# A gated linear attention with an MLP behind it: k of the first unit moves to SyncE's queue, and the first two v loads arrive as bf16

## The chip, the core and the metric

The kernel runs on one core of a Trainium2 chip. The metric is the device time of one execution in microseconds (us). Six kinds of hardware matter here. TensorE (PE in the profile) multiplies matrices, and its weight loads have a row of their own, PEld. VectorE (DVE) and ScalarE (ACT) work on elements. GpSimd (POOL) does little arithmetic here, but it issues most of the loads. SyncE (SP) issues loads and stores. Sixteen DMA engines move the data of all queues.

## The reference, cut to what matters

There are two stages. The first is a recurrent attention over 768 steps for 4 batches of 8 heads, with a decay `alpha` for each channel of the state. The second is an MLP with a tanh GELU over the 3072 tokens that come out.

```python
for t in range(S):                       # B, H, S, D = 4, 8, 768, 48
    state = alpha[:, :, t, :, None] * state + einsum('bhd,bhe->bhde', k[:, :, t], v[:, :, t])
    y[:, :, t] = einsum('bhd,bhde->bhe', q[:, :, t], state)
x = y.transpose(0, 2, 1, 3).reshape(B * S, H * D)      # 3072 x 384
h = x @ w_in                                           # 384 x 2048
out = gelu_tanh(h) @ w_out                             # 2048 x 384
```

All inputs and the output are float32.

## The kernel before

**Chunks, pairs and units.** The 768 steps are cut into six chunks of 128. A chunk of two batches is a pair, so there are twelve pairs, numbered 0 to 11; pairs 0 and 1 are chunk 0 of batches 0 and 1, and of batches 2 and 3. One batch of a pair is called a unit here. A task's name is its kind, the pair and a running number: `kp0.0` is the task `kp` of the first unit of pair 0, `kp0.1` that of the second unit.

**What a unit does.** Its decays go through a logarithm (`ln`, ACT), a running sum by a triangular matrix (`cum`, PE) and exponentials (`b`, `binv`, `bend`, ACT). VectorE forms `qp` = q times b and `kp` = k times binv (line 451). TensorE transposes both (`t`, line 461), ACT or DVE copies them out of PSUM (`ev`, line 479), TensorE forms the scores (`attn`, line 555), and VectorE masks them (`mask`, line 562). Then TensorE multiplies the masked scores with v (`y`, line 612), and the transposed-back keys with v (`kv`, line 572), from which VectorE makes the state (`st`, line 597). The result is copied (`x`), transposed (`tx`, line 643) and copied again (`xe`, line 647), and is then the input of the MLP: `l1` (line 655, weights `w_in`), `gelu` (ACT) and `l2` (line 674, weights `w_out`).

**Order.** Each engine runs its instructions in a fixed order. For the opening this order is written out by hand in `FIRST`: each word has an engine letter (P TensorE, V VectorE, A ScalarE, G GpSimd, S SyncE) and a task. `P:fill.3` is three products of zeros that keep TensorE running. After the list a planner orders the rest with costs and due times. TensorE's opening goes, cut to what matters, `cum0.0 cum0.1 t0.0 t0.1 attn0.0 t0.2 t0.3 t0.4 attn0.1 t0.5 cum1.0 y0.0 kv0.0 cum1.1 tx0.0 y0.1 t1.1 t1.0 kv0.1 tx0.1 attn1.0 t1.2 l10.0`. An instruction that waits holds up all that stand behind it on its engine.

**The loads.** There are two ways in. `RINGS` lists the twelve loads of a, q and k of pairs 0 and 1, one batch each, 192 KB; SP issues them, or ACT those named in `BY_ACT`. They are numbered `load.0` to `load.11` in the order of `RINGS`: a0.0, a0.1, q0.0, k0.0, q0.1, k0.1, then the same of pair 1. These are hardware queues: q1 in the profile is SP's, q10 is ACT's. All other loads, those of v and of the weights among them, are issued by GpSimd on a software queue, q0, in the order of `LOADS`. This queue can change the type on the way, and the weights and most v loads come as bf16 by it. The names of the first ones are `load.12` (v of pair 0), `load.13` (`w_in` part 0), `load.14` (v of pair 1), `load.15` to `load.17` (`w_in` parts 1 to 3) and then `w_out`. Two `gate` tasks hold GpSimd back: `load.12` may go once a0.1 has landed (`gate.0`), and what stands behind it once k0.1 has landed (`gate.1`); a gate is a small copy on GpSimd that reads the loaded tile (line 338).

**v.** For the pairs in `NARROW` v is loaded as float32 into a buffer of the pool `a`, and four `vb` tasks (line 422), one for each unit, copy it to a bf16 tile of the pool `vb`. For all other pairs the load itself writes the `vb` tile. In `load`, the line that decides is

```python
t = "vb" if n == "v" and u["m"] not in self.NARROW else n
u[t] = self.tile("a" if t == "v" else t, [C, 2, H, D], BF16 if t == "vb" else F32, t)
```

where `u["m"]` is the pair. `LANDED` holds times that the planner takes for the landings; it is the same in both kernels.

Of the kernel before, what the change touches and what calls it, by code (L numbers as in the profile page):

```python
# [174 lines left out]
class _Kernel:  # L175
# [8 lines left out]
    PACKED, CUM_FF, R = (0, 1), (0, 1), 4  # L184
    RINGS = (('a', 0, 0, 1), ('a', 0, 1, 2), ('q', 0, 0, 1), ('k', 0, 0, 1), ('q', 0, 1, 2), ('k', 0, 1, 2),
             ('a', 1, 0, 1), ('a', 1, 1, 2), ('q', 1, 0, 1), ('k', 1, 0, 1), ('q', 1, 1, 2), ('k', 1, 1, 2))
    BY_ACT = (2, 3,)

    FIRST = """
        A:table.0 A:load.2 A:load.3 S:load.0 S:load.1 S:load.4 A:ln0.0 S:load.5 P:fill.7 P:cum0.0 A:ln0.1 G:gate.0 G:load.12 S:load.6 P:cum0.1 A:b0.0 S:load.7  # L190
        A:bend0.0 V:qp0.0 A:binv0.0 A:binv0.1 S:load.8 V:kp0.0 P:fill.2 P:t0.0 A:b0.1 V:ev0.0 P:fill.1 P:t0.1 S:load.9 A:ev0.1 V:qp0.1 S:load.10 A:bend0.1
        P:fill.3 P:attn0.0 V:kp0.1 G:gate.1 S:load.11 P:t0.2 G:load.13 V:mask0.0 A:ev0.2 P:t0.3 G:load.14 V:mask0.1 A:ev0.3 P:fill.1 P:t0.4 V:ev0.4 P:fill.1
        P:attn0.1 A:ln1.0 G:load.15 P:t0.5 V:mask0.3 P:cum1.0 A:ev0.5 G:load.16 V:vb0.0 A:ln1.1 V:end0.0 P:y0.0 V:mask0.2 G:load.17 P:kv0.0 A:binv1.0 P:cum1.1
        V:st0.0 A:x0.0 G:load.18 A:vb0.1 V:kp1.0 P:tx0.0 A:b1.0 P:y0.1 V:xe0.0 G:load.19 V:qp1.0 P:t1.1 A:x0.1 A:bend1.0 G:load.20 A:b1.1 P:fill.1 P:t1.0
        A:ev1.0 V:ev1.1 G:load.21 V:qp1.1 P:fill.1 P:kv0.1 V:st0.1 G:load.22 A:binv1.1 P:tx0.1 P:attn1.0 V:xe0.1 G:load.23 P:t1.2 V:kp1.1 P:l10.0 A:ev1.2
        G:load.24 V:mask1.0 P:t1.3 A:bend1.1 P:t1.4 V:mask1.1 G:load.25 A:ev1.3 P:l10.1 V:ev1.4 G:load.26 A:vb1.0 P:t1.5 P:attn1.1 G:load.27 V:ev1.5 P:y1.0
        G:load.28 P:l10.3 V:end1.0 V:vb1.1 V:mask1.2 G:load.29 A:gelu0.0 P:kv1.0 P:l10.2 V:mask1.3 A:x1.0 G:load.30 P:l10.5 A:gelu0.1 V:st1.0 A:gelu0.3 P:y1.1
        G:load.31 P:l10.4 A:gelu0.5 V:x1.1 P:tx1.0 A:gelu0.2 P:tx1.1 P:l10.6 G:load.32 V:xe1.1 A:gelu0.4 V:xe1.0 P:l10.7 A:gelu0.6 G:load.33 P:l11.0 A:gelu0.7
        P:l11.6 A:gelu1.0 P:l11.5 A:gelu1.6 P:l11.7 A:gelu1.5 P:l11.2 A:gelu1.7 P:l11.4 A:gelu1.2 P:l11.3 A:gelu1.4 P:l11.1 A:gelu1.3 P:kv1.1 P:l20.0
        A:gelu1.1 P:l20.4 P:l20.1 A:ln2.0 P:l20.2 P:cum2.0 P:l20.5 A:b2.0 A:binv2.0 P:l20.9 A:bend2.0 V:kp2.0 A:ln2.1 P:l20.6 V:st1.1 P:cum2.1 V:qp2.0 P:l20.8  # L200
# [8 lines left out]
              27900, "load.23": 28300, "load.24": 30100, "load.25": 31000, "load.26": 31900, "load.27": 32600, "load.28": 32900, "load.29":  # L209
              34800, "load.30": 36700, "load.31": 38400, "load.32": 41200, "load.33": 42600}  # L210

    NARROW = (0, 1)

    TURN_QK = (7,8,9,10,11)

# [101 lines left out]
    def load(self, n, c, i, lo=0, hi=2):  # L317
# [4 lines left out]
        def emit(e):  # L322
            t = "vb" if n == "v" and u["m"] not in self.NARROW else n
            if t not in u:
                u[t] = self.tile("a" if t == "v" else t, [C, 2, H, D], BF16 if t == "vb" else F32, t)
            dma = {"SP": nc.sync, "ACT": nc.scalar}.get(e, nc.gpsimd).dma_start
            src = self.src[n][2 * i + lo:2 * i + hi]
            if u["packed"] and n != "v":
                dma(u[n][:, lo].rearrange("p (o r) d -> p o (r d)", o=2),
                    src[0, :, c * C:(c + 1) * C].rearrange("h (g r) d -> g h (r d)", r=R))  # L330
            else:
                dma(u[t][:, lo:hi].rearrange("t b h d -> t (b h) d"), src.rearrange("b h s d -> s (b h) d")[c * C:(c + 1) * C])  # L332
# [369 lines left out]
    def tasks(self):  # L702
# [9 lines left out]
        def load(key, cost, emit):  # L712
            nonlocal n
            land = W[key[1] if key[0] == "w" else "cast" if key[0] == "v" and key[1] not in self.NARROW else "strip"]
            loads[key] = s.add("load", {"POOL": cost}, n, emit, gate, land=land * 3 // 8 if key[0] != "w" and key[1] in self.SPLIT else land)
# [17 lines left out]
        for r, m, lo, hi in self.RINGS:  # L733
            loads[r, m, lo] = loads[r, m, hi - 1] = s.add(
                "load", {"ACT" if n in self.BY_ACT else "SP": W["ring_issue"]}, n, self.load(r, *pairs[m], lo, hi), land=(W["ring_v" if r == "v" else "ring"] * (hi - lo) // 2 if n else W["begin"]))
            n += 1
# [22 lines left out]
        for m, (c, i) in enumerate(pairs):  # L759
# [61 lines left out]
            vin = [loads["v", m, j] for j in range(2)]  # L821
            if m in self.NARROW:
                vin = [s.add("vb", {"DVE": W["vb"], "ACT": W["vb_act"]}, P + 19, self.narrow(u, j, j + 1), vin[j:j + 1]) for j in range(2)]
# [87 lines left out]
            kp[0].take("kp", *tq, *kvs)  # L911
            if m in self.NARROW:
                loads["v", m, 0].take("a", *vin)
# [129 lines left out]
```

## Time and profile before

| | us |
|---|---|
| median of 3 runs | 175.16 (174.92 to 175.46) |
| the profiled execution | 175.79 |
| its span, first to last instruction | 174.0 |
| PE busy in the span | 168.1 (97%) |
| ACT, DVE, POOL busy | 129.2, 95.0, 58.2 |
| PE busy from 0 to 17 us | 14.11 of 17 |
| DMA: 28.88 MB in the span | mean 166 GB/s |

The times of the profile are counted from the start of the span. 1.8 us of the profiled execution lie outside of it, and this execution was 0.6 us longer than the median. The clock that TensorE was granted is full (1.00) in every stretch. A busy PE counts the products of zeros too, 17 of which stand in the opening. The opening lasts until the first product of the MLP, which starts 17.06 us into the span.

The landings of the opening's loads, as issue time plus time to landing in the trace's list of DMA issues, each asked for in a window around its issue:

| load | issued by, at | lands at | first read |
|---|---|---|---|
| a0.0, a0.1 | SP 0.74, 1.4 | 3.7, 4.7 | `ln0.0` 3.74, `ln0.1` 4.75 |
| q0.0 | ACT 1.20 | 4.2 | `qp0.0` 5.77 |
| k0.0 | ACT 1.92 | 7.5 | `kp0.0` 7.57 |
| q0.1, k0.1 | SP 2.19, 2.86 | 7.7, 8.2 | `qp0.1` 8.65, `kp0.1` 9.11 |
| v of pair 0 | POOL 4.90 | 11.5 | `vb0.0` 12.24 |
| `w_in` part 0 | POOL 8.79 | 14.8 | `l10.0` 17.06 |
| v of pair 1 | POOL 9.52 | 16.0 | `vb1.0` 18.62 |
| `w_in` part 1 | POOL 10.71 | 18.3 | `l10.3` 19.68 |
| `w_in` part 2 | POOL 11.5 | 20.5 | `l10.5` 21.2 |
| `w_in` part 3 | POOL 12.2 | 22.2 | `l10.6` 23.03 |

### The profile page before, as it was taken

To read this page: it belongs to the slowest core of one execution; us is meant where nothing else is said; L and a number is where in the kernel's file an instruction comes from. 1 tells how busy PE (TensorE), PEld (TensorE's weight loads), DVE (VectorE), ACT (ScalarE), POOL (GpSimd) and SP (SyncE) were. 2 spreads that over 40 slices of the span, in tenths; PEclk is the share of its full clock that TensorE was granted. 3 is DMA by queue.
4 is the path that set the end of the run, shared out by engine and by line. 5 is a ranking of instruction groups with operands and counts; after the bars stand their busy time and mean duration, and the time that the engine had idled before them with its cause. 6 is when DMAs were issued, how large, how long until landed. Compare 5 with 4: busy or idle time off the path is not lost.

```text
span 174.0 us, 4688 instructions
## 1 busy us (share of the span) xinstructions
PE 168.1 (97%) x1973; PEld 132.2 (76%) x1973; DVE 95.0 (55%) x188; ACT 129.2 (74%) x217; POOL 58.2 (33%) x67
## 2 busy tenths in 40 slices
PE   7799999999999999999999999999999999999993
PEld 2466999666887896797698697788697796886973
DVE  6399920265967864865995866587464520420000
ACT  4578999765979759959889697968799693481931
POOL 2398346995735667572000028000203000000000
PEclk9999999999999999999999999999999999999999
DMA  4999999999999999999952367999895843202102
GB/s 138 292 271 217 201 247 227 234 223 203 238 285 194 241 254 221 231 235 192 214 162 52 98 160 177 161 172 161 77 138 100 88 127 86 92 23 68 49 0 90
DMA packets 49621, 28.88 MB, mean 166 GB/s; under 512 B 37696, under 2 KB 46016, under 8 KB 49600
## 3 DMA queue, kind: packets, MB, share of 16 engines
q0 software_dynamic: 26464, 17.70, 62.6%
q1 hardware_dynamic: 22592, 10.49, 26.1%
q10 hardware_dynamic: 544, 0.39, 0.9%
q8 instruction: 15, 0.25, 0.7%
q14 instruction: 6, 0.05, 0.1%
HBM read 25.17 MB, written 4.72 MB: 172 GB/s over the span
## 4 chain that ended last, share of the span: by engine, by line
PE 86%; DMA 8%; ACT 3%; DVE 0%; issue 0%; SPq 0%; DVEq 0%
PE hT L655 36%; PE acc L674 33%; DMA xT<-x 5%; PE at L555 3%; DMA k<-in_k_dram 3%; PE qkT_ps L461 2%; PE cum L411 2%; PE yps L620 2%; PE kv L572 1%; PE qkT_ps L492 1%; PE yps L535 1%; PE xT_ps L643 1%; PE yps L612 1%; ACT qkT L479 1%; PE k_ps L507 1%; ACT L304 1%
## 5 line engine op out<-in xcount | busy, mean ns | idle before, releaser
L655 PE MATMUL hT<-xT,w_in 128*128 128x256 bf16 x576 | 68.3, 273 | 0.4 <-DMA xT<-x 0.4
L674 PE MATMUL acc<-w_out,gT 128*128 128x384 bf16 (+3 forms) x416 | 68.7, 313 | 0.0
L661 ACT ACTIVATE gT<-hT 128x512 bf16<-128x512 f32 x96 | 55.3, 601 | 13.1 <-PE hT L655 9.7
L655 PEld LDWEIGHTS <-w_in 128*128 128x128 bf16 x576 | 61.3, 114 | 2.6 <-DMA xT<-x 0.8
L674 PEld LDWEIGHTS <-gT 128*128 128x128 bf16 x416 | 37.0, 98 | 19.4
L562 DVE TENSOR_TENSOR atm<-at,ut 128x512 bf16<-128x512 f32 x48 | 30.2, 684 | 19.1 <-PE at L555 18.9
L686 ACT COPY ot<-acc 128x384 f32<-128x384 f32 (+3 forms) x18 | 7.9, 442 | 16.7 <-PE acc L674 15.9
L451 DVE TENSOR_TENSOR kp<-k,binv 128x768 bf16<-128x768 f32 (+1 forms) x15 | 11.9, 791 | 11.8 <-ACT binv L440 10.6
L346 POOL CAST gate<-qkT 128x1 f32<-128x1 bf16 x3 | 0.6, 183 | 45.0 <-DMA qkT<-kp 45.0
L332 POOL DMA_DIRECT2D k<-in_k_dram x11 | 12.2, 1107 | 8.4 <-DMA vb<-in_v_dram 4.4
L451 DVE TENSOR_TENSOR qp<-q,b 128x768 bf16<-128x768 f32 (+1 forms) x15 | 11.9, 793 | 4.4 <-ACT b L440 4.3
L332 POOL DMA_DIRECT2D vb<-in_v_dram x11 | 12.1, 1104 | 6.0 <-DMA w_in<-in_moe_w_in_dram 1.5
L332 POOL DMA_DIRECT2D a<-in_alpha_dram x11 | 12.2, 1113 | 4.9 <-DMA w_in<-in_moe_w_in_dram 1.3
L332 POOL DMA_DIRECT2D q<-in_q_dram x11 | 12.2, 1109 | 4.0 <-DMA w_out<-in_moe_w_out_dram 1.0
L440 ACT ACTIVATE b<-cum 128x768 bf16<-128x768 f32 (+1 forms) x15 | 10.3, 684 | 3.2 <-PE cum L411 1.6
L304 ACT ACT_TABLE_LOAD x9 | 11.5, 1283 | 0.9 <-PEq L1027 0.7
L630 DVE CAST x<-yps 128x384 bf16<-128x384 f32 x10 | 5.4, 556 | 12.2 <-PE yps L620 12.2
L661 ACT ACT_TABLE_LOAD x9 | 11.5, 1283 | 0.2
L594 DVE TENSOR_TENSOR stmp<-kv,st 128x384 f32<-128x384 f32 x16 | 8.9, 553 | 4.8 <-PE kv L572 4.7
L440 ACT ACTIVATE binv<-cum 128x768 bf16<-128x768 f32 (+1 forms) x15 | 10.3, 684 | 0.1
L597 DVE TENSOR_TENSOR st<-stmp,ends 128x384 bf16<-128x384 f32 x16 | 8.9, 558 | 0.6
L479 ACT COPY qkT<-qkT_ps 128x512 bf16<-128x512 bf16 (+1 forms) x8 | 5.4, 693 | 4.6 <-PE qkT_ps L461 4.5
(79 smaller groups left out, 155.2 us busy)
## 6 DMA issues: line engine op xcount, KB each, us to landing
out_dram<-ot SPq DMA_DIRECT2D x19, 192.0 KB, 4.2
a<-in_alpha_dram POOLq DMA_DIRECT2D x9, 384.0 KB, 11.8
q<-in_q_dram POOLq DMA_DIRECT2D x9, 384.0 KB, 11.2
k<-in_k_dram POOLq DMA_DIRECT2D x9, 384.0 KB, 11.5
vb<-in_v_dram POOLq DMA_DIRECT2D x9, 192.0 KB, 11.4
w_in<-in_moe_w_in_dram POOLq DMA_DIRECT2D x4, 384.0 KB, 8.3
w_out<-in_moe_w_out_dram POOLq DMA_DIRECT2D x4, 384.0 KB, 11.0
out_dram<-ot SPq DMA_DIRECT2D x9, 96.0 KB, 3.2
```

Of the source, the lines that this page charges most:

```text
L304: nc.scalar.add_instruction(mybir.InstLoadActFuncSet(name=nc.get_next_instruction_name(), act_func_set_id=i, engine=mybir.EngineType.Activ ...
L332: dma(u[t][:, lo:hi].rearrange("t b h d -> t (b h) d"), src.rearrange("b h s d -> s (b h) d")[c * C:(c + 1) * C])
L440: self.nc.scalar.activation(u[n].rearrange("t i h d -> t i (h d)")[:, lo:hi], cum, AF.Exp, scale=1.0 if n == "b" else -1.0)
L451: self.nc.vector.tensor_tensor(out, rows, b, op=ALU.mult)
L479: self.copy(e)(t, ps)
L562: self.nc.vector.tensor_tensor(u["atm", i][:, o], u["at", i][o], self.ut[:, None, :].to_broadcast([self.C, self.H // 2, self.C]), op=ALU.mult)
L594: nc.vector.tensor_tensor(s, acc, old, op=ALU.add)
L597: nc.vector.tensor_tensor(new.rearrange("f p (o d) -> f (p o) d", o=2), acc.rearrange("f p (o d) -> f (p o) d", o=2), ends, op=ALU.mult)
L655: self.nc.tensor.matmul(h[:, s], w_in[:, j, nt % 4 + s], self.xT[c % self.NX][:, j, lo:hi].rearrange("p g t -> p (g t)"), start=j == 0, st ...
L661: return lambda e: self.nc.scalar.activation(self.gT[c % self.NG][:, nt:nt + 2, lo * self.C:hi * self.C], f.pop(("h", c, lo, nt)), AF.Gelu ...
L674: self.nc.tensor.matmul(f["acc", c, b][:, lo:hi], self.gT[c % self.NG][:, nt, b * self.C:(b + 1) * self.C], self.w_out[:, nt, lo:hi], star ...
L686: self.copy(e)(f["ot", c, b][:, sl], f["acc", c, b] if half is None else f["acc", c, b, half][:, sl])
```

## The change

Two things change. `BY_ACT` loses load 3, so k0.0 is issued by SP, third in its queue: behind the two alpha loads of pair 0 and ahead of q0.1. ACT's queue has one load left, q0.0. `NARROW` is empty, so the v loads of pairs 0 and 1 write bf16 tiles themselves, and the four `vb` tasks are gone: two of VectorE (`vb0.0`, `vb1.1`) and two of ScalarE (`vb0.1`, `vb1.0`). The words `A:load.3` and those of the four `vb` tasks leave `FIRST`, and `S:load.3` enters it; the rest of it is the same.

```diff
-    BY_ACT = (2, 3,)
+    BY_ACT = (2,)
     FIRST = """
-        A:table.0 A:load.2 A:load.3 S:load.0 S:load.1 S:load.4 A:ln0.0 ...
+        A:table.0 A:load.2 S:load.0 S:load.1 S:load.3 S:load.4 A:ln0.0 ...
...
-        P:attn0.1 A:ln1.0 G:load.15 P:t0.5 V:mask0.3 P:cum1.0 A:ev0.5 G:load.16 V:vb0.0 A:ln1.1 V:end0.0 P:y0.0 ...
+        P:attn0.1 A:ln1.0 G:load.15 P:t0.5 V:mask0.3 P:cum1.0 A:ev0.5 G:load.16 A:ln1.1 V:end0.0 P:y0.0 ...
-        V:st0.0 A:x0.0 G:load.18 A:vb0.1 V:kp1.0 ...
+        V:st0.0 A:x0.0 G:load.18 V:kp1.0 ...
...
-        ... A:ev1.3 P:l10.1 V:ev1.4 G:load.26 A:vb1.0 P:t1.5 P:attn1.1 G:load.27 V:ev1.5 P:y1.0
+        ... A:ev1.3 P:l10.1 V:ev1.4 G:load.26 P:t1.5 P:attn1.1 G:load.27 V:ev1.5 P:y1.0
-        G:load.28 P:l10.3 V:end1.0 V:vb1.1 V:mask1.2 ...
+        G:load.28 P:l10.3 V:end1.0 V:mask1.2 ...
...
-    NARROW = (0, 1)
+    NARROW = ()
```

What follows from it on each queue: TensorE has the same instructions in the same order, and `y0.0`, `y0.1` and `y1.0`, which waited for the `vb` tasks, now wait for the DMA. SP issues eleven loads in the opening instead of ten, ACT one instead of two. GpSimd issues the same loads; since v of pairs 0 and 1 takes no buffer of the pool `a` any more, the v load of pair 7 stands four places earlier, ahead of the alpha, q and k loads of pair 8 and the alpha load of pair 9, and some of its waits are for other loads or engines.

## The prediction

> **What bounds the kernel now.** I read the busy times by stretch first, then the chain of waits, then the timeline of the opening, and last the list of DMA issues. The stretches (us, then busy time of PE, PEld, DVE, ACT and POOL, granted clock, DMA share, GB/s) are
>
> ```profile
> 0.00:17.00 17.00, 14.11 (x150) 8.37 (x151) 12.45 (x42) 10.74 (x24) 10.54 (x21) 1.00 0.92 231
> 17.00:24.00 7.00, 7.00 (x95) 6.68 (x93) 5.58 (x13) 6.49 (x13) 2.52 (x4) 1.00 1.17 204
> ```
>
> From 17 us on TensorE is full, and it stays so nearly to the end: its only listed wait after 17 us is 0.4 us. So the program ends a fixed time after `l10.0` starts (17.06), and the change is worth what it moves that start by, unless the MLP then waits for its weights. The DMA engines are full too, so a load that gains takes from another. The chain of waits (start, length, what) runs through k0.0:
>
> ```profile
> 1.92 5.55 DMA k<-in_k_dram
> ...
> 7.57 0.57 DVE kp L451
> 8.14 0.05 issue
> 8.19 0.40 PE qkT_ps L461 x4
> ...
> 13.71 0.42 ACT vb L422
> 14.13 0.04 issue
> 14.18 0.36 PE yps L612 x8
> ```
>
> It shows both targets of the change: a 5.55 us load, and a 0.42 us narrowing. The timeline (start, length, engine, line, instruction) has what stands around them:
>
> ```profile
> 4.90 1.29 POOL L332 DMA_DIRECT2D v<-in_v_dram  x1
> ...
> 12.24 0.35 DVE L422 CAST vb<-v 128x384 bf16<-128x384 f32 x1
> ...
> 12.41 0.24 PE L383 MATMUL cum<-blk,la 128*128 128x4 f16 x4
> ...
> 12.65 0.37 PE L612 MATMUL yps<-vb,atm 128*128 128x48 bf16 x8
> ```
>
> v of pair 0 takes 6.6 us to landing, to 11.5. `y0.0` starts at 12.65, where `vb0.0` (to 12.59) and the product before it on TensorE (12.41 + 0.24) end together. After the change the load itself must be there.
>
> **Part 1: k0.0 by SP.** SP issues it at 2.19, where q0.1 was, and each of its later loads 0.66 us later (the step between two issues). On ACT one issue of 0.63 us goes, which lay beside its wait for a0.0 until 3.74: nothing. Now k0.0 shares the engines with q0.1, which lands only 0.2 us after it (7.7): from 5 to 7.4 us the list of queues has 140 packets of ACT's queue beside 796 of SP's. Alone behind a0.1, k0.0 should land before q0.1 has moved. But the stretch is slow: 936 packets in 2.4 us, 390 per us, against 711 in 1.5 us, 474 per us, from 3.0 to 4.5. Bounds: no gain (landing 7.5), and `kp0.0` right behind `qp0.0` (5.77 + 0.56), at 6.4 instead of 7.57, a gain of 1.2. I take 0.55 (landing about 6.9), near the middle, since the engines are slow there. `qp0.1`, `kp0.1` (k0.1 lands at 8.2 as before: the same six loads lie ahead), `attn0.0`, `ln1.0` and `cum1.0` follow on DVE, PE and ACT, so `y0.0` could start at 12.1. `gate.1` hangs on k0.1 and stays, and with it the issue of `w_in`. The loads of pair 1 keep their place: SP's later issues are hidden by a queue that is full until 12.8.
>
> **Part 2: the four copies go.** `vb0.0` (0.35, DVE) ended with the product before `y0.0`: nothing by itself, it is what lets the 0.55 through. `vb0.1` (0.53 busy, 0.42 on the chain) stood before `b1.0` on ACT (to 14.51); but `qp1.0` also waits on DVE for `xe0.0` (14.17 + 0.35 = 14.52), so 0.03 at most comes through there. `vb1.0` (0.52, ACT) stood before the GELU's table load; the gelus then trail TensorE, which waits for none of them: nothing. `vb1.1` (0.35, DVE) lies in a stretch where DVE is busy 5.58 of 7: nothing.
>
> **Part 3: v by casting.** This is where it turns. The float32 v load moves in large pieces, a casting load in pieces of 96 bytes. Three answers on DMA queues (packets, MB, share of 16 engines) show it: v of pair 0 beside SP's queue (8.2 to 10.6), a casting v load late in the span with nothing beside it (135 to 136), and casting loads beside SP's stores (47.2 to 47.8).
>
> ```profile
> q0 software_dynamic: 108, 0.39, 55.1%
> q1 hardware_dynamic: 468, 0.34, 51.1%
> ```
>
> ```profile
> q0 software_dynamic: 1390, 0.13, 251.4%
> ```
>
> ```profile
> q1 hardware_dynamic: 110, 0.15, 81.8%
> q0 software_dynamic: 111, 0.03, 40.1%
> ```
>
> 108 packets carry 0.39 MB in the first; a whole casting load has 2059 packets (134.4 to 136.6), 129 per engine against 7. Alone that is no loss: 1390 in 1.0 us on 16 engines is 11.5 ns each, 1.5 us a load. But beside a full queue the packets alternate one by one, 110 to 111. From 8.2 to 13.3 SP's queue still moves 979 packets, 61 per engine, at 33 ns (335 packets in 0.7 us, 10.6 to 11.3). So 7 large packets wait for 7 of SP's, and 129 small ones for all 61: 61 x (33 + 11.5) = 2.7 us, then 68 x 11.5 = 0.8, together 3.5. The first packets of the load move from 8.2 on, and not on all engines at once; from 8.6 the last moves at 12.1. Landing was 0.9 us behind that end (10.6 to 11.5), so v lands at 13.0. Bounds: 11.5 (as now), and 14.4: in the third answer a pair takes 0.6 x 16 / 111 = 86 ns, and SP's packets there are twice as large (0.15 MB / 110), so 66 of it are theirs and 20 are left for a small one; 61 x 53 + 68 x 20 = 4.6 us, from 8.9, and 0.9. I take 13.1, by the sum, since the rows with these very packet sizes give it. `y0.0` goes then: 13.15 against 12.65, a loss of 0.5, and the 0.55 of part 1 is used up in waiting. Behind the waiting `y0.0` on TensorE stand `kv0.0`, `cum1.1`, `tx0.0`, `y0.1`; DVE's `st0.0` and so `kp1.0`, `xe0.0`, `qp1.0` wait for them, `attn1.0` for these, and `l10.0` starts at 17.56.
>
> The Trainium skill's DMA: Bandwidth & Descriptors (Queues, rings and completion order) says that an engine drains a whole packet, typically 9 to 17 descriptors, before it turns to the next queue. If 9 of these pieces went at a turn, v would need 129 / 9 = 14 turns of 33 + 104 ns, 2.0 us, land at 11.5, and the opening would gain; the 110 to 111 above speaks against it. Its table of specifications asks for 512 bytes or more per transfer for full rate, which speaks against the change; alone the load costs 1.5 us, so the row shows little of that loss.
>
> **Part 4: the queue behind v.** `w_in` part 0 began to move at 11.3 and now waits until about 12.1; SP's queue is then done, so some of the 0.8 comes back. v of pair 1 has the engines nearly to itself and costs 1.5; the float32 load moved 0.39 MB, at the 262 GB/s of 13.3 to 15.3 also 1.5. I take +0.7 for `w_in` parts 1 to 3, between 0 (no engine does more work) and 2.0 (0.8, and 129 x 20 - 1500 ns, 1.1, for the second load). Part 2 lands at 20.5 and is read at 21.2, part 3 at 22.2 and 23.03: slack 0.7 and 0.8, and 0.5 more with the later start. So nothing is lost in the taken case; at +2.0 it would be 0.7. But it also caps any gain: an opening that starts `l10.0` earlier runs into weights that land later. v of pair 1 (16.0, then 16.8) is read at 19.47. The v load of pair 7 that moves ahead of four loads is issued some 68 us in, for a stage that starts 30 us later: nothing; the loads that it passes move by one issue, 1.15 us, and are read later still.
>
> **Sum.** -0.55 (k0.0), 0 (the copies), +1.05 (v: from 12.1 to 13.15), 0 (`w_in`): +0.5 on the execution shown, 175.8 to 176.3. That execution was 0.6 over the median, so 175.16 becomes 175.7.
>
> **Rivals.**
> *Faster: v is in time.* If the small packets get a larger share, or move as soon after the issue as the late load did (132.51 to 134.4, 1.9 us, against 3.3), v lands by 12.1, and `y0.0` starts 0.55 earlier. For it: the late load's 4.3 us to landing. Against: moved sooner, it meets more of SP's packets. `w_in` part 2 caps it at 0.7 less its delay. Most of the 0.55 then comes through, 174.6; it decides below a landing of 12.1.
> *Same: the two cancel.* v lands at 12.6 to 12.8, or 13.1 with some of `vb0.1` returned: 175.3.
> *Slower by more.* v lands at 14.4: 14.45 - 12.65 = 1.8, so 177.0. For it: the 20 ns. Against: the late load's 11.5.
> *k0.0 lands no earlier*, since the engines are slow from 5 to 7.4: then the 0.55 is missing, but as v is later than 12.65 nothing changes: 175.7.
>
> **How the numbers follow.** A measurement can tell about 0.3% (0.53 us) from no change. v late (with either k0.0): 0.45, of which 0.31 above that bound, as `w_in` can only add to the loss, and 0.14 below it; later still: 0.22; cancelled: 0.14; in time: 0.19. So faster 0.19, same 0.14 + 0.14 = 0.28, slower 0.31 + 0.22 = 0.53. The range reaches from the rival in time (174.6) to a little above the late one (177.3).
>
> **What would show it.** k0.0 lands near 6.9 and `kp0.0` starts near 7.0; the page's count of packets grows by some 4,000; TensorE waits about 1 us for v ahead of `y0.0`, which starts near 13.15; `l10.0` starts near 17.6; `w_in` part 3 lands near 22.9. Wrong it would be if v lands before 12.1, if TensorE stalls on `w_in` ahead of `l10.5` or `l10.6`, or if the stages after 24 us change in length.

## The result and the profile after

The changed kernel takes 177.92 us in the median of 20 executions (175.55 to 179.64), the kernel before 175.3 in as many beside it (174.62 to 178.83). The ratio is 1.0111, with a 95% interval of 1.0081 to 1.0140: slower by 1.95 us, between 1.4 and 2.45. The medians, 2.6 us apart, are over all executions, while the ratio compares the faster state alone and leaves out seven of the changed kernel's (178.3 us and more). The forecast was slower in direction, and too small: 175.16 to 175.7, in a range that ended at 177.3. Counted from the same 175.16, 1.95 us give 177.1, just inside that range. The profiled execution of the changed kernel took 177.81 us with a span of 176.0, against 175.79 and 174.0.

The same stretches as before, with the same columns (us, busy PE, PEld, DVE, ACT, POOL, clock, DMA share, GB/s):

```profile
0.00:17.00 17.00, 13.35 (x136) 8.20 (x139) 11.38 (x39) 10.14 (x23) 9.81 (x20) 1.00 1.16 200
17.00:24.00 7.00, 7.00 (x100) 6.47 (x100) 5.50 (x13) 6.00 (x12) 2.91 (x4) 1.00 1.19 208
```

TensorE is 0.76 us less busy in the opening (13.35 against 14.11), and the DMA engines are busier (1.16 against 0.92) while they move less (200 against 231 GB/s). From 17 us on TensorE is full again. The chain of waits (start, length, what) now runs through v of pair 0 instead of k0.0:

```profile
1.54 3.17 DMA a<-in_alpha_dram
...
4.76 0.12 POOL gate L338
4.88 8.44 DMA vb<-in_v_dram
13.32 0.14 issue
13.46 0.36 PE yps L612 x8
```

The load that took 6.6 us as float32 takes 8.44 by the casting queue and lands at 13.32. The page's line for the software queue (packets, MB, share of 16 engines) had 26464 packets before and has 3904 more:

```profile
q0 software_dynamic: 30368, 17.30, 64.7%
```

In the timeline, `kp0.0` starts at 6.85 instead of 7.57, so k0.0 did come earlier:

```profile
6.85 0.55 DVE L451 TENSOR_TENSOR kp<-k,binv 128x384 bf16<-128x384 f32 x1
```

TensorE's waits (total, times, longest) name the two places where it stands still:

```profile
PE yps L612 <- DMA vb<-in_v_dram: 1.5, 1, 1.5
PE hT L655 <- DMA xT<-x: 1.4, 1, 1.4
```

The first is `y0.0`, waiting for v. The second lies near 115 us, and before it was

```profile
PE hT L655 <- DMA xT<-x: 0.4, 1, 0.4
```

I set the starts of the same instructions of both profiles against each other: the changed kernel is 0.72 us behind when the MLP is full (24 us), 1.02 from about 44 us on, and 2.01 from 115 us to the end. So there were three pieces to explain: 0.72 in the opening, 0.30 at 43 us, and 1.0 at 115 us, of which the prediction had only the first.

Later profiles use the same measure: "delay" is how far a kernel's instructions are behind those of the profile before, at the time named.

### The profile page after: what moved, and what is told of

It reads as the page before. It is cut to its first block, busy times and chain, and to the rows that moved or that the text cites. A ratio compares the mean times of both kernels' runs of the same rounds, so it can differ in the third digit from the quotient of the medians.

```text
span 176.0 us, 4681 instructions
## 1 busy us (share of the span) xinstructions
PE 168.2 (96%) x1971; PEld 132.5 (75%) x1973; DVE 94.4 (54%) x186; ACT 128.6 (73%) x215; POOL 58.3 (33%) x67
## 4 chain that ended last, share of the span: by engine, by line
PE 83%; DMA 12%; ACT 1%; DVE 1%; issue 1%; SPq 1%; POOL 0%
PE hT L655 36%; PE acc L674 32%; DMA xT<-x 5%; DMA vb<-in_v_dram 5%; PE at L555 3%; DMA a<-in_alpha_dram 2%; PE cum L411 2%; PE yps L620 2%; PE kv L572 2%; PE qkT_ps L492 1%; PE xT_ps L643 1%; PE yps L535 1%; PE qkT_ps L461 1%; PE yps L612 1%; PE cum L413 1%
## 5 line engine op out<-in xcount | busy, mean ns | idle before, releaser
L661 ACT ACTIVATE gT<-hT 128x512 bf16<-128x512 f32 x96 | 55.4, 600 | 14.4 <-PE hT L655 10.9
L451 DVE TENSOR_TENSOR kp<-k,binv 128x768 bf16<-128x768 f32 (+1 forms) x15 | 11.9, 791 | 10.6 <-ACT binv L440 10.6
L332 POOL DMA_DIRECT2D vb<-in_v_dram x13 | 14.6, 1124 | 5.3 <-DMA w_in<-in_moe_w_in_dram 1.7
L630 DVE CAST x<-yps 128x384 bf16<-128x384 f32 x10 | 5.4, 556 | 12.3 <-PE yps L620 12.3
L394 ACT ACTIVATE la<-a 128x768 f16<-128x768 f32 (+1 forms) x11 | 8.5, 785 | 0.1
## 6 DMA issues: line engine op xcount, KB each, us to landing
a<-in_alpha_dram POOLq DMA_DIRECT2D x9, 384.0 KB, 11.6
vb<-in_v_dram POOLq DMA_DIRECT2D x11, 192.0 KB, 11.6
```

Source lines behind the costliest of these rows:

```text
L394: self.nc.scalar.activation(u["la"][:, lo:hi, :, 0:self.D], u["a"][:, lo:hi], AF.Ln)
L451: self.nc.vector.tensor_tensor(out, rows, b, op=ALU.mult)
L661: return lambda e: self.nc.scalar.activation(self.gT[c % self.NG][:, nt:nt + 2, lo * self.C:hi * self.C], f.pop(("h", c, lo, nt)), AF.Gelu ...
```

## The experiments

### One part at a time

`e1_k_only` has only the move of k0.0, `e2_v_only` only the casting loads. The other two have the move and one casting load each: `e3_v0_cast` that of pair 0, `e4_v1_cast` that of pair 1.

```diff
# e1_k_only, against the kernel before
-    BY_ACT = (2, 3,)
+    BY_ACT = (2,)
-        A:table.0 A:load.2 A:load.3 S:load.0 S:load.1 S:load.4 ...
+        A:table.0 A:load.2 S:load.0 S:load.1 S:load.3 S:load.4 ...
# e2_v_only, against the kernel before; the four words of the vb tasks leave FIRST
-    NARROW = (0, 1)
+    NARROW = ()
# e3_v0_cast: as e1, and the words V:vb0.0 and A:vb0.1 leave FIRST
+    NARROW = (1, )
# e4_v1_cast: as e1, and the words A:vb1.0 and V:vb1.1 leave FIRST
+    NARROW = (0, )
```

> k0.0 goes to SP's queue, v of both pairs stays float32 and is narrowed on chip. Theory (the loss is the late casting load of pair 0, and k0.0 alone is a gain): k0.0 lands near 6.7 as in the changed kernel, v of pair 0 near 11.5, kp0.0 starts near 6.9, y0.0 near 12.1, and the program is 0.3 to 0.6 us faster than before. Rival 1 (the move of k0.0 itself does harm, since all of the opening then goes through one hardware queue): 0.5 to 1 us slower. Rival 2 (an earlier opening runs into w_in, which lands when it did): 0 to 0.2 us faster, with a wait of TensorE on w_in ahead of l10.5 or l10.6.

> v of pairs 0 and 1 by casting loads, k0.0 stays on ACT's queue. Theory: v of pair 0 lands near 13.3 whichever queue k0.0 takes, y0.0 starts near 13.4, and the time is that of the changed kernel, 1.5 to 2.3 us over before. Rival (k0.0 on SP's queue makes that queue longer, and this is what holds v up): v lands before 12.5 and the loss is under 0.5 us.

> k0.0 on SP's queue, v of pair 0 by a casting load, v of pair 1 as float32 and narrowed on chip; the v load of pair 7 then stands where it stood before. Theory: all of the loss is in pair 0's load, so l10.0 starts 0.7 later than before and the time is that of the changed kernel (1.5 to 2.3 us over before). Rival (a part of the loss comes from the other order of GpSimd's late loads, or from pair 1's load): 0.7 to 0.9 us over before, the opening's share alone.

> k0.0 on SP's queue, v of pair 0 as float32 and narrowed on chip, v of pair 1 by a casting load; the v load of pair 7 stands four places earlier, as in the changed kernel. Theory: pair 1's load has slack, so this is the kernel with k0.0 alone: 0.2 to 0.6 us faster than before. Rival (the other order of the late loads or pair 1's load costs 1.2 us): 0.6 to 1 us slower than before.

All four ran beside 35 executions of the kernel before (175.29 in the median).

| kernel | `kp0.0` | `y0.0` | `l10.0` | delay at 24 us | wait for xT at 114 us | median, us | ratio, 95% |
|---|---|---|---|---|---|---|---|
| before | 7.57 | 12.65 | 17.06 | 0 | 0.4 | 175.29 | |
| e1_k_only | 6.74 | 11.85 | 16.22 | -0.71 | 1.8 | 175.57 | 1.0017 (0.9974 to 1.0060) |
| e2_v_only | 6.88 | 13.02 | 17.34 | +0.28 | 0 | 176.0 | 1.0026 (0.9982 to 1.0071) |
| e3_v0_cast | 6.94 | 12.47 | 16.79 | -0.25 | 0.4 | 177.01 | 1.0083 (1.0044 to 1.0122) |
| e4_v1_cast | 6.71 | 12.79 | 17.12 | +0.29 | 0 | 175.45 | 1.0019 (0.9977 to 1.0061) |
| the change | 6.85 | 13.46 | 17.78 | +0.72 | 1.4 | 177.92 | 1.0111 (1.0081 to 1.0140) |

Three things follow. The move alone helps the opening by 0.7 to 0.8 us, as its theory had it, and yet the 0.3 to 0.6 us that were expected in the time are not there. Its wait for xT shows where the gain went in that execution, and that was not what I had expected:

```profile
PE hT L655 <- DMA xT<-x: 1.8, 1, 1.8
```

The casting load of pair 1 costs nothing that can be measured, though the gain expected of `e4_v1_cast` is missing too. In its profile v of pair 0, which is float32 there, landed only at 12.35 us and held `y0.0` up to 12.79; in that of `e1_k_only` the same load landed at 10.94. So with k0.0 on SP's queue v can be late without casting as well.

The loss needs the casting load of pair 0 *and* k0.0 on SP's queue: with the casting loads and k0.0 on ACT the kernel is 0.46 us slower, which is within its interval, where I had expected 1.5 to 2.3 (v landed at 12.89 in its profile, between what the theory and the rival wanted). The two parts are not additive: 0.3 and 0.46 by themselves, 1.95 together. The trace shows one thing that they do to each other. Here are the DMA queues while the pieces of v of pair 0 move, first in the changed kernel (7.2 to 12.95 us), then in `e2_v_only` (8.3 to 12.5 us):

```profile
q0 software_dynamic: 2153, 0.29, 74.7%
q1 hardware_dynamic: 1425, 1.03, 64.8%
```

```profile
q0 software_dynamic: 2247, 0.39, 118.5%
q1 hardware_dynamic: 736, 0.53, 41.4%
```

The same 2048 pieces share the engines with 1425 packets of SP's queue in the one, and with 736 in the other. k0.0 puts 256 more packets in front of SP's later loads, so more of these lie beside v. That is 256 of the 689; most of the rest comes from v itself, which was issued later in `e2_v_only` (5.47 against 4.88 us), because `gate.0` opened later, and found more of SP's packets gone. That these packets are what makes v late is argued and not shown: between the first and the last piece of v, the changed kernel has 1420 of them and its v landed at 13.32, `e3_v0_cast` has 1204 and 12.33, `e10_after_pad` (below) 1142 and 14.10.

The profile of `e3_v0_cast` looks better than the kernel is: that execution took 175.6 us, the shortest of its runs (175.6 to 180.05), and v landed at 12.33. How far v's landing varies comes below.

### v of pair 0 in two loads

`e5_v0_halves` is the changed kernel with v of pair 0 as two casting loads, one for each batch.

```diff
-            for lo, hi in ((0, 2),) if m in self.PACKED else self.parts(m):
+            for lo, hi in ((0, 1), (1, 2)) if (m, names) == (0, 'v') else ((0, 2),) if m in self.PACKED else self.parts(m):
# FIRST and LANDED: G:load.13 follows G:load.12; the later loads are numbered one higher
```

> The changed kernel, but v of pair 0 comes by two casting loads, one for each batch, the first unit's ahead. Theory (the small packets take turns with those of SP's queue, one by one, so half of them are through in about half the time): the first half lands near 11, y0.0 starts at 11.9 to 12.2 without a wait, y0.1 no later than in the changed kernel, l10.0 at 16.6 to 17.2, and the program is 0.5 to 1.2 us faster than the changed kernel. Rival (v is late because a casting load starts or ends late, whatever its size): the first half lands after 12.5 and the time is that of the changed kernel.

It takes 176.36 us against 175.87 beside it, a ratio of 1.0033 (0.9997 to 1.0069). That is the theory's side: most of the loss is gone. The timeline shows that the first unit no longer waits, and the second hardly:

```profile
11.66 0.36 PE L612 MATMUL yps<-vb,atm 128*128 128x48 bf16 x8
...
13.49 0.36 PE L612 MATMUL yps<-vb,atm 128*128 128x48 bf16 x8 [0.24 <-DMA vb<-in_v_dram]
```

The second half (13.36) does not land earlier than the undivided load did in the first profile. Its opening gains 1.03 us by 20 us (the masks of VectorE; 0.76 at `l10.0`), and at 24 us only 0.29 of that is left: the MLP meets its weights and the GELUs. `w_in` parts 2 and 3 land at 20.70 and 22.66, and products of the MLP start at 20.75 and 22.71. That is the cap that the prediction put on any gain.

### A delay by itself

These two put idle products on TensorE ahead of `y0.0` in the kernel before, so that the opening is late while no load changes. `e6_delay_only` has four, `e9_delay_match` six, to reach the start that v had given `y0.0` in the changed kernel.

```diff
-        ... V:vb0.0 A:ln1.1 V:end0.0 P:y0.0 V:mask0.2 ...
+        ... V:vb0.0 A:ln1.1 V:end0.0 P:fill.6 P:y0.0 V:mask0.2 ...
```

> The kernel before, with four more products of zeros on TensorE right ahead of y0.0, 0.86 us of work: this imitates the late v alone, with all loads as they were. Theory A (the later part of the loss, at the transposes of x near 105 us, comes with any start of the MLP that is this late): 1.5 to 2.2 us over before, with a wait of TensorE of over 1 us for xT near 115. Theory B (that part comes from the changed loads or is chance of one profile): l10.0 0.8 later and the program 0.7 to 1.0 us over before.

> The kernel before with six idle 128x512 products (216 ns each) put directly ahead of y0.0 on TensorE, nothing else: v of the first pair still comes as float32. Four of them left y0.0 at 13.00 us and the run at +0.3 us; six should put y0.0 at 13.4 to 13.5 us, where v by the casting queue puts it. Theory (a wait of this length in the opening costs its own length, and the rest of what the change costs is made by later stages and not by the delay): 0.6 to 0.9 us over the kernel before, ACT's x2.1 near 43 us starts normally. Rival (a delay of 0.7 us shifts every later stage against its loads, and the wait for xT of pair 7 near 114 us grows by about 1 us with it): 1.6 to 2.1 us over the kernel before, with that wait at 1.4 us or more.

Four products moved `y0.0` only to 13.00, since k0.0 landed earlier in that execution (`kp0.0` at 7.19): +0.26 at 24 us, and 175.97 against 175.87, ratio 1.0013 (0.9982 to 1.0044). That was too small a dose to decide. Six did it:

```profile
12.10 1.46 PE L313 MATMUL idle<-zero 128*128 128x512 bf16 x6
13.39 0.36 PE L612 MATMUL yps<-vb,atm 128*128 128x48 bf16 x8
```

`y0.0` starts at 13.39, 0.07 from the changed kernel's start, and `l10.0` at 17.71 against 17.78. The time is 175.95 against 175.23, ratio 1.0031 (1.0009 to 1.0052), so about 0.55 to 0.7 us. All twelve executions lie between 175.56 and 176.19, while those of the changed kernel spread over 4 us. A delay of this size costs about its own length (0.65 at 24 us in its profile) and is not multiplied by later stages; the wait for xT did not grow with it (there was none). So the 1.95 us had to be something else: v later than in the first profile, or the later pieces, or something that comes of a TensorE that waits, since here it was kept busy.

### The stage at 114 us

In the profiles the wait for xT of pair 7 looked like 1 us of the loss. xT comes by four transposing DMAs, which SP issues while GpSimd's loads of pairs 10 and 11 fill the engines. `e7_before_held` and `e8_after_held` hold back the loads k10, a11, q11 and k11 until xT of pair 7 has landed, in the kernel before and in the changed one.

```diff
-            t = self.xT[c % self.NX][:, 0, 2 * i + 1, 0:1] if n == "x" else ...
+            t = self.xT[0][:, 0, 3, 0:1] if (n, m) == ("k", 8) else self.xT[c % self.NX][:, 0, 2 * i + 1, 0:1] if n == "x" else ...
# and GpSimd's tasks from that gate on are written out behind the transposes
```

> The kernel before, but GpSimd's gate ahead of its last loads of k of pair 10 and a, q, k of pair 11 reads the transposed x of pair 7 instead of the transposed k of pair 8, so that these four loads start only when that x has landed. Theory (the transposes of x near 105 us are slow because they share the engines with these loads): xT lands within 3 us of its issue, TensorE doesn't wait for it, the times of the runs lie closer together, and the median is 0 to 0.4 us under before. Rival (the four loads are then late for pair 11): slower by 1 us or more, with waits on DMA after 115 us.

> The changed kernel with the same change to the gate. Theory (about 0.7 us of the loss arise in the opening and the rest at the transposes of x near 105 us): 0.6 to 1.0 us over the kernel before with that gate, and 0.8 to 1.5 us faster than the changed kernel. Rival (the rest of the loss arises elsewhere): 1.7 us or more over the kernel before with that gate.

Here the rival was right. The wait for xT disappeared in both (the shortest transpose in that stretch took 2.3 us instead of 5.5 in the kernel before), but the loads that were held were then late for the stages behind, and both kernels lost: 179.53 (ratio 1.0171, 1.0111 to 1.0232) and 181.72 (1.0258, 1.0200 to 1.0315) against 175.87. TensorE's first wait in `e7_before_held` shows the new one:

```profile
PE at L555 <- DMA qkT<-kp: 1.7, 1, 1.7
```

So the transposes and the loads do compete, and holding these loads only moves the wait. The pair can't say what the wait is worth between the two kernels, since the new waits differ (2.2 us instead of the expected 0.6 to 1.0). The opening of `e8_after_held` repeats that of the changed kernel: TensorE waited 1.56 us for v, `l10.0` at 17.75. A part of its long time is not waiting: in its profile TensorE's granted clock is half (0.50) from 128.2 to 135.1 us.

### Both kernels again, and ACT's instruction count

At 43 us, ACT's copy `x2.1` started 0.37 us after the semaphore event that it waited for, in place of 0.06. Across the profiles so far it did so where ACT's stream had 255 records (the change, `e5`, `e8`) and not where it had 256 to 258. `e10_after_pad` therefore puts three small copies into the changed kernel's ACT stream; `e11_after_again` and `e12_before_again` are the changed kernel and the kernel before, unchanged.

```diff
# e10_after_pad, against the changed kernel; pad is a new constant tile of 128x16
-            t.emit(t.engine)
+            t.emit(t.engine), t.name in ("load.2", "x0.0", "ev1.3") and nc.scalar.copy(self.pad[:, 0:2], self.half)
```

> The changed kernel with three copies of 128x2 elements on ACT: one after its first load, two where the two removed narrowing copies of ACT stood, so that ACT has as many instructions as in the kernel before; the other engines' orders are the same. Theory (x2.1's 0.37 us between the semaphore event and its start belongs to the place of the instruction in ACT's stream): x2.1 starts 0.06 us after its event again, the difference to the kernel before stays at +0.6 to +0.9 us from 24 us to 105 us instead of growing to +1.0 at 44 us, and the time is 0.3 us under that of the changed kernel. Rival (it belongs to the timing of that moment): x2.1 starts 0.3 us late again and the time is that of the changed kernel within 0.2 us.

> The changed kernel once more, for a second profile of the wait for xT of pair 7. Theory (the length of that wait varies from execution to execution, and only the delay of the opening and the 0.3 us at 43 us belong to the change): 1.0 to 1.4 us over the kernel before in the profile up to 105 us, the wait anywhere from 0 to 1.8 us, and the time 1.0 to 2.0 us over. Rival (the wait is 1 us longer in the changed kernel every time): 1.4 us or more of wait again, 1.8 to 2.2 us over.

> The kernel before once more, against itself: what two identical kernels differ by. Theory (the wait for xT of pair 7 varies by execution): its profile has 0 to 1.8 us of it, and the time is within 0.3 us of the kernel before. Rival (the wait is fixed by the kernel): 0.3 to 0.5 us of wait again.

| kernel | v lands | `y0.0` | `l10.0` | delay at 24 us | at 44 us | at the end | wait for xT | median, us | ratio, 95% |
|---|---|---|---|---|---|---|---|---|---|
| e12_before_again | 11.6 | 12.30 | 16.72 | -0.34 | -0.34 | -0.13 | 0.6 | 175.19 | 0.9989 (0.9959 to 1.0019) |
| e11_after_again | 14.29 | 14.43 | 18.75 | +1.69 | +1.99 | +2.20 | 0.6 | 178.0 | 1.0135 (1.0086 to 1.0183) |
| e10_after_pad | 14.11 | 14.24 | 19.42 | +2.35 | +2.35 | +1.76 | 0 | 176.88 | 1.0062 (1.0024 to 1.0100) |

`e11_after_again` is the run that settles the main question. The same kernel, and v lands a whole microsecond later than in its first profile. From its chain and its waits:

```profile
4.96 9.33 DMA vb<-in_v_dram
14.29 0.14 issue
14.43 0.36 PE yps L612 x8
```

```profile
PE yps L612 <- DMA vb<-in_v_dram: 2.5, 1, 2.5
...
PE hT L655 <- DMA xT<-x: 0.6, 1, 0.6
```

The wait for xT, which the rival wanted at 1.4 again, is 0.6, as in the kernel before beside it. The theory's 1.0 to 1.4 us up to 105 us were missed as well, because v came so late. Between these two profiles the loss can be followed without a rest: 2.03 us at 24 us (1.69 and 0.34), 2.33 at 44 us, 2.33 at the end. The opening makes 2.03 and ACT's start 0.30; the stage at 114 us makes nothing. In the profiles of all kernels the wait for xT was 0.4, 1.4, 1.8, 0, 0.4, 0, 1.0, 0.4, 0, 0, 0.6 and 0.6 us (before, the change, e1 to e6, e9 to e12), so it varies as much between executions as between kernels. That the first pair of profiles had 1.0 us more of it in the changed kernel was, as far as one repeat can tell, not a property of the change.

For ACT, here are the event and the start of `x2.1` in the changed kernel, then in `e11_after_again`, then with the three copies (the times behind the durations are the first and the last start):

```profile
L636 ACTq EVENT_SEMAPHORE  x1: 17/17/17, 43.3 to 43.3; - x1
L636 ACT CAST x<-yps x1: 478/478/478, 43.7 to 43.7; 128x384 bf16<-128x384 f32 x1
```

```profile
L636 ACTq EVENT_SEMAPHORE  x1: 17/17/17, 44.3 to 44.3; - x1
L636 ACT CAST x<-yps x1: 478/478/478, 44.7 to 44.7; 128x384 bf16<-128x384 f32 x1
```

```profile
L636 ACTq EVENT_SEMAPHORE  x1: 17/17/17, 45.0 to 45.0; - x1
L636 ACT CAST x<-yps x1: 478/478/478, 45.0 to 45.0; 128x384 bf16<-128x384 f32 x1
```

The late start is back in the repeat, a microsecond later on the clock, and gone with the copies (45.02 behind 44.96), where the delay stays at 2.35 from 24 to 105 us. That it doesn't grow is the theory's outcome, not the timing of a moment; the 2.35 itself is far over the 0.6 to 0.9 expected. The whole time is no clean test of the 0.3 us: `e10_after_pad` came out 1.1 us under its twin beside it, more than this can explain, although one of its copies stood on the opening's critical stretch (0.20 us of ACT ahead of `b1.0`) and its MLP started 0.67 us later in the profile. Its profile had no wait for xT; what its other runs had isn't known.

The late MLP of that profile has a cause of its own, which the other profiles of the changed kernel don't show. Soon after the wait for v TensorE's granted clock is half for 3.41 us (same columns as above, the clock third from the end):

```profile
15.68:19.09 3.41, 2.98 (x33) 2.29 (x30) 2.76 (x7) 1.92 (x5) 1.78 (x2) 0.50 1.32 205
```

From `y0.0` to `l10.0` it takes 5.18 us, against 4.32 in both profiles of the changed kernel. One such stretch brings the mean clock of an execution to 0.99. Seven of the 20 executions of the changed kernel have that mean, three of the six of `e11_after_again`, three of ten of `e10_after_pad` and three of the twelve of `e3_v0_cast`. The 60 of `e1`, `e2`, `e4`, `e5` and `e9` have none, and the kernel before has five in the 85 beside the experiments and one in the twelve of `e12_before_again`. The seven of the changed kernel take 178.43 us in the median, the other thirteen 177.41. So the lower clock is a part of the loss in some executions. That it comes of the wait for v is likely, and not shown; where in the other executions it lies isn't known.

## Why the prediction was right in direction and too small

**The opening bounds the kernel, and v turns it: right.** TensorE waits for v ahead of `y0.0`, and no other wait of the opening grew by more than 0.3 us. The packets grew by 3904 where 4000 were forecast, `kp0.0` starts at 6.85 where 7.0 was, and the next instruction could have started at 11.93 (`cum1.0` ends) where 12.1 was. No wait for `w_in` appeared, and `e5_v0_halves` showed the cap that it puts on a gain.

**"I take 13.1, by the sum" (v's landing): the term that was too small.** It landed at 13.3, 13.3, 14.1 and 14.3 in the four profiles of the changed kernel or of kernels with its opening (the change, e8, e10, e11), and at 12.3 in `e3_v0_cast`, whose loads are the same up to that one. The term of +1.05 measures 1.5 to 2.5 us as TensorE's wait in the first four. That the first profile came within 0.3 us of the sum was luck, as two of its parts were off in opposite directions: the last piece started at 12.8 to 13.8 where the sum had 12.1, and the landing came 0.4 to 0.5 us behind it where the sum had 0.9. The sum treated all sixteen engines alike, 129 pieces and 61 packets each, one by one. The packets of the trace look different. Of the 2048 pieces of v, these had started:

| kernel | half | 1950 | the last | landed |
|---|---|---|---|---|
| the change | 9.6 | 11.7 | 12.9 | 13.3 |
| e11_after_again | 9.7 | 12.6 | 13.8 | 14.3 |
| e10_after_pad | 9.8 | 11.8 | 13.7 | 14.1 |
| e2_v_only | 9.6 | 11.3 | 12.5 | 12.9 |

From 8.2 to 10.6 us the changed kernel moves almost three pieces for each packet of SP's queue, not one, so the bulk is faster than I had it (1272 against 461):

```profile
q0 software_dynamic: 1272, 0.12, 98.0%
q1 hardware_dynamic: 461, 0.33, 56.5%
```

How many go at a turn such counts can't tell. The prediction held its 110 to 111 packets against the skill's 9 to 17 at a turn, but turns of any length give equal counts if both queues take turns of the same length.

Landing is set by the last 98 pieces, which need another 1.2 us and more (1.9 in e10) while `w_in` already moves, whose first packet starts at 11.7. A mean over the engines can't give that time. That some engines lag behind the others is the likely reason, and not shown. The Trainium skill's DMA: Bandwidth & Descriptors (Queues, rings and completion order) says that each pair of a queue and an engine has a ring of its own; the trace doesn't name the engine of a packet, so no run here can show which one lags, or why. The sum also counted SP's packets as they were in the kernel before, as if the two parts did not meet: `e2_v_only` against the change has nearly twice as many of them beside v with k0.0 on SP's queue (736 and 1425). The upper bound of 14.4 held in every profile, and the rival that was worked from it, 177.0, came nearest.

**"The program ends a fixed time after `l10.0` starts": not exact.** 0.30 us are added at 43 us in every profile of the changed kernel's ACT stream. The four copies were costed at nothing by the work that hid them, and this was right for their busy time; that three instructions fewer on ACT would put a later one in another place was not thought of. And the wait for xT near 114 us moves single executions by up to 1.8 us either way. It also means that an earlier opening is not always paid out, as in `e1_k_only`.

**The -0.55 of k0.0: right, and worth nothing by itself.** Its landing went from 7.5 to about 6.7, and 6.2 to 6.6 in the other profiles with it on SP. On ACT it varied: `kp0.0` started at 7.57, 7.50, 7.22, 7.19, 7.15 and 6.88 (before, e7, e12, e6, e9, e2), so the profile before was the upper end of a range. The mean of these is 7.25, and on SP's queue it is 6.80: of the 0.72 us between the two first profiles some 0.3 were this execution's.

**The sum again**, with what was measured. Against the kernel before, the opening's delay was 0.72 and 1.69 us in the two profiles of the changed kernel, and the one of the kernel before was itself 0.34 late against its own repeat; with the 0.30 of ACT, that is 1.0 to 2.3 us, and the measured 1.95 lies in it. In executions with a stretch at half clock it is more: 0.86 us in the profile of `e10_after_pad`, a term that the prediction didn't have. I have two profiles of each; how v's landing is spread over all executions isn't known. That it makes most of the spread of the times (175.55 to 179.64) is argued from the tight times of `e9_delay_match`, where TensorE was kept busy, and not shown; the clock is not all of it, as the thirteen executions at full clock spread from 175.55 to 179.12.

## What to carry to other kernels

A load that is cut into many small pieces lands when the last of them has moved, so beside a full queue price it by the last per cent of its pieces and not by the mean rate, and count the neighbour queue's packets as they will be after the change. Two edits that each do no harm that can be measured can meet on the same engines: try them apart and together. Look at the granted clock of every execution, and not only of the profiled one: a stretch at half clock behind a long wait may be missing from the profile. Before a difference of a microsecond late in two profiles is explained, take each profile a second time: here 1.0 us of the first comparison was only the execution.

## What the hardware showed besides

**A start of ACT depends on its place in the stream.** In all fourteen profiles, `x2.1` starts 0.37 us after its event exactly where ACT's stream has 255 records (the change, e5, e8, e11), and 0.05 to 0.06 us after it where it has 256, 257 or 258. In those same four, the second packet of 8 KB after the start on queue q14, which the page lists as instruction, moves at 46.3 to 48.3 us; in the other ten it moves at 32.8 to 35.4. So the cause is likely the loading of instructions, which I did not test further. The Trainium skill's Runtime: NRT & Kernel Launch (Instruction fetch mechanics) says that instructions are refilled block by block while the engine runs, at a cost that is mostly hidden; if that is the cause, 0.3 us of it was not hidden here.

**Identical kernels differ by place.** The same casting load of the same kernel landed at 13.32 and at 14.29 us, and the same k0.0 on ACT let `kp0.0` start anywhere from 6.88 to 7.57. The second of the four transposing DMAs of xT of pair 7's stage took 7.97, 8.19, 8.18, 8.96 and 9.38 us to land in five profiles (before, e12, e11, the change, e1), of which the first two and the next two are of identical kernels.
